# The first piece's block-diagonal copies, all on VectorE instead of shared with ScalarE

## The chip, the cores and the metric

The kernel runs on one core of a Trainium2 chip. Its metric is the device time of one launch, in microseconds (us). The engines of a core have their own instruction queues and work them off in order: PE (TensorE, matrix products; PEld is its weight load), DVE (VectorE), ACT (ScalarE), POOL (GpSimd) and SP, which here only issues DMA transfers. An instruction that needs another engine's result waits on a semaphore, and everything behind it in its own queue waits with it.

## The reference

A chunked scan (a state-space layer with decay) over 4 batches of 8 heads and 768 positions is followed by two feed-forward layers over 3072 tokens of width 256 with 2048 hidden features:

```python
for c in range(nc):                       # chunks of 32 positions
    L = np.exp(cum[:, :, :, None] - cum[:, :, None, :]) * causal
    M = np.einsum('bhin,bhjn->bhij', Cc, Bc) * L
    y_intra = np.einsum('bhij,bhjd->bhid', M, xc)
    y_inter = np.einsum('bhin,bhnd->bhid', Cc, state) * np.exp(cum)[..., None]
    y[:, :, sl] = y_intra + y_inter
    state = decay_full * state + np.sum(Bx, axis=2)
...
h = x @ w_in;   x = np.maximum(0.01 * h, h) @ w_out       # first layer
h = np.maximum(x @ w2_in, 0.0);   return h * h @ w2_out   # second layer
```

## The kernel before

**The scan.** The 3072 tokens are taken as 12 pieces of 256 positions (`scan_piece`, p from 0 to 11). A piece holds 8 heads as 2 groups of 4; the 4 heads lie on the four 32-partition quadrants of the 128 partitions. So that one matrix product serves four heads, operands are laid out block-diagonally: the nested function `diag` (L314 to L320) copies each quadrant of a source into its own column block of a 128 x 128 matrix, 16 such matrices side by side. There are four such arrays per piece: `kbd` from `kmx` (keys), `xbh` and `xbl` from `xh` and `xl` (the high and low halves of x), `sbd` from the transposed states. For pieces 1 to 11 the four copies of an array are DMAs. For piece 0 they are instructions: quadrants 0 and 1 on VectorE, 2 and 3 on ScalarE.

The chain of a piece: scales (squares on ACT at L235, a small product on PE at L290, some tiny DVE instructions from L298), decays by scans on DVE (L189, L195), `kbd` and `xbh`, products S on PE (L348, L349), the mask on DVE (L358), `mkh` on ACT (L360) and `mkl` on DVE (L365), products Y on PE (L373 to L375), states (ACT L377, DVE scan L213, ACT L382, DVE L384 and transpose L386), `sbd`, products L393 and L394, and the piece's result as a high half `yh` (ACT L397) and a low half `yl` (DVE L398).

**The layers.** The tokens go through both layers in 8 blocks, four of one piece and four of two. Each block has 16 hidden tiles of 128 features, taken two at a time in a small block. `hmm` (L417) makes `hp` on PE from `yl`, `yh` and the weights; `act` makes `gh` and `t` on ACT (L435, L436) and `gl` on DVE (L441); `omm` (L445) adds up the outputs `o`. Piece 0's `yl` releases block 0's first `hp`, and piece 1's `yl` block 1's first `hp`.

**The weights** arrive as 64-bit words and are split into two parts while the first pieces run. Of every chunk `wst` (512 KB, 32 chunks; 8 of them are w1i) ACT runs L130 and L133, DVE L141 and L142, ACT L153 (the high part, as `wh1i`) and DVE L154 (the low part, as `wl1i`).

**What sets the order.** The program is written as one sequence: the first piece's scan, eight rounds of weight splitting, then blocks with scan steps in between (`step_to`). From it the language's scheduler settles at build time which instruction stands where on each engine. Where an instruction is put on another engine, instructions far from it can change places too.

Of the kernel before, what the change touches and what calls it, by code (L numbers as in the profile page):

```python
# [45 lines left out]
def ssd_moe_kernel(ctx: ExitStack, tc: tile.TileContext, in1, in2, w1i, w1o, w2i, w2o, out):  # L46
# [6 lines left out]
    nc = tc.nc  # L53
# [254 lines left out]
    def scan_piece(p, tiles, get_y):  # L308
# [5 lines left out]
        def diag(dst, src):  # L314
            for h in range(4):
                d, v = dst[quad[h], :, h, :], src[quad[h]]
                if p > 0:
                    nc.sync.dma_start(d, v)  # L318
                else:
                    (nc.vector.tensor_copy if h < 2 else nc.scalar.copy)(d, v)  # L320

        him = sp.tile([P, U, T], F16, tag="f0", name="him")
        ch = sp.tile([P, U, T], F16, tag="f2", name="ch")
# [6 lines left out]
        cl = sp.tile([P, U, T], F16, tag="f3", name="cl")  # L330
        nc.vector.scalar_tensor_tensor(kmx, bt_t, sb, him, ALU.mult, ALU.subtract)
        diag(kbd, kmx)
        xh = sp.tile([P, U, D], F16, tag="xh", name="xh")
        nc.scalar.activation(xh, x_t, AF.Copy, scale=sx)
# [5 lines left out]
        xl = sp.tile([P, U, D], F16, tag="xl", name="xl")  # L340
        nc.vector.scalar_tensor_tensor(xl, x_t, sx, xh, ALU.mult, ALU.subtract)
        diag(xbh, xh)
        yield
        mkh = sp.tile([P, U, T + N], F16, tag="mkh", name="mkh")
        mkl = sp.tile([P, U, T + N], F16, tag="mkl", name="mkl")
        S = pz.tile([P, U, T], F32, tag="S", name="S")
        for u in range(U):
# [6 lines left out]
            mk[:, :, T:], b_t, sb, lt[:, :, T - 1 : T].to_broadcast([P, U, N]), ALU.mult, ALU.mult  # L354
        )
        diag(xbl, xl)
        yield
        nc.vector.scalar_tensor_tensor(mk[:, :, :T], S, kk, lt, ALU.mult, ALU.mult)  # L358
# [261 lines left out]
```

## Time and profile before

| | |
|---|---|
| Runs | 635.60, 636.33, 636.08 us; median 636.08 us |
| Profiled execution | 637.78 us, of which the span of the profile is 636.1 us |
| PE busy | 586.2 us, 92% of the span |
| PEld busy | 516.9 us, 81% |
| DVE busy | 402.6 us, 63%, 687 instructions |
| ACT busy | 372.9 us, 59%, 678 instructions |
| POOL busy | 5.2 us, 1% |

Shares over the whole span hide the stages. The page's row of 40 slices shows DVE and ACT at 9 tenths or more in the first slices, where PE is at 0 to 9, and PE at 9 in nearly all slices after the first third, where DVE and ACT are at 3 to 6. The chain of waits on the page gives PE 76%, ACT 9%, DVE 6% and DMA 6% of the span.

### The profile page before, as it was taken

How to read it: one execution, taken by the hardware profiler on the slowest of the kernel's cores; microseconds unless marked ns; L12 is line 12 of the kernel's file. 1: busy time of each engine (PE TensorE's matmuls, PEld its weight loads, DVE VectorE, ACT ScalarE, POOL GpSimd, SP SyncE). 2: the span in 40 equal slices, each digit the busy share in tenths (PEclk: the TensorE clock that was granted, in tenths of full speed). 3: DMA queues.
4: the chain of work that ended last, by engine and by line, in shares of the span. 5: the costliest groups of instructions: out<-in, count | busy, mean ns of one | idle time of the engine just before them, and what ended most of it. 6: DMA issues, size and time to landing. Idle time of an engine off the chain costs nothing.

```text
span 636.1 us, 11298 instructions
## 1 busy us (share of the span) xinstructions
PE 586.2 (92%) x4434; PEld 516.9 (81%) x4434; DVE 402.6 (63%) x687; ACT 372.9 (59%) x678; POOL 5.2 (1%) x14
## 2 busy tenths in 40 slices
PE   0297698999989999999999999999999999999997
PEld 0287698989989888899988888888888888888885
DVE  6999999995558664576564576564565322555553
ACT  6999998876555545545545555455544433544442
POOL 3000000000000000000000000000000000000000
PEclk9999898999989999999999999999999999999999
DMA  7886565555351412202212212212000000000000
GB/s 272 275 291 195 139 205 98 174 124 127 105 94 40 74 51 26 50 35 42 51 51 26 49 36 25 51 67 26 9 1 9 34 1 1 0 2 0 34 1 33
DMA packets 111396, 46.47 MB, mean 73 GB/s; under 512 B 94320, under 2 KB 101104, under 8 KB 111344
## 3 DMA queue, kind: packets, MB, share of 16 engines
q1 hardware_dynamic: 111344, 45.76, 27.8%
q8 instruction: 35, 0.57, 0.4%
q14 instruction: 17, 0.14, 0.1%
HBM read 36.83 MB, written 3.15 MB: 63 GB/s over the span
## 4 chain that ended last, share of the span: by engine, by line
PE 76%; ACT 9%; DVE 6%; DMA 6%; issue 2%; SPq 1%; DVEq 0%; ACTq 0%
PE o L453 12%; PE hp L425 12%; PE hp L427 12%; PE hp L426 12%; PE o L458 12%; PE o L454 12%; DMA all<-in 2%; DMA in<-in 2%; ACT wst L130 1%; ACT wst L133 1%; ACT sq L235 1%; SPq L318 1%; ACT t L436 1%; ACT gh L435 1%; DVE e L195 1%
## 5 line engine op out<-in xcount | busy, mean ns | idle before, releaser
L441 DVE TENSOR_TENSOR gl<-t,gh 128x512 fp32r<-128x512 f32 x192 | 132.3, 689 | 139.5 <-ACT t L436 85.9
L435 ACT ACTIVATE gh<-hp 128x512 fp32r<-128x512 f32 x96 | 57.2, 596 | 84.1 <-PE o L454 75.6
L425 PE MATMUL hp<-yl,wh1i 128*128 128x256 f32 (+1 forms) x256 | 89.5, 350 | 10.8 <-DVE yl L398 4.6
L440 ACT CAST gh<-t 128x512 fp32r<-128x512 f32 x96 | 59.5, 620 | 66.3 <-DVE t L439 56.2
L439 DVE TENSOR_TENSOR t<-t 128x512 f32<-128x512 f32 x96 | 66.2, 689 | 43.4 <-ACT t L438 43.1
L438 ACT ACTIVATE t<-hp 128x512 f32<-128x512 f32 x96 | 57.4, 598 | 56.7 <-PE hp L427 54.5
L453 PE MATMUL o<-gh,wl1o 128*128 128x256 f32 (+1 forms) x256 | 84.9, 347 | 4.5 <-DVE wl1o L154 3.6
L426 PE MATMUL hp<-yh,wh1i 128*128 128x256 f32 (+1 forms) x256 | 88.6, 346 | 0.0
L427 PE MATMUL hp<-yh,wl1i 128*128 128x256 f32 (+1 forms) x256 | 88.4, 345 | 0.0
L426 PE MATMUL hp<-yh,wh2i 128*128 128x256 f32 (+1 forms) x256 | 86.0, 336 | 0.0
L425 PE MATMUL hp<-yl,wh2i 128*128 128x256 f32 (+1 forms) x256 | 86.0, 336 | 0.0
L427 PE MATMUL hp<-yh,wl2i 128*128 128x256 f32 (+1 forms) x256 | 86.0, 336 | 0.0
L453 PE MATMUL o<-gh,w2o 128*128 128x256 f32 (+1 forms) x256 | 83.6, 343 | 1.6 <-DVE yl L467 1.5
L454 PE MATMUL o<-gh,wh1o 128*128 128x256 f32 (+1 forms) x256 | 83.0, 340 | 0.0
L454 PE MATMUL o<-gh,w2o 128*128 128x256 f32 (+1 forms) x256 | 81.9, 336 | 0.0
L425 PEld LDWEIGHTS hp<-yl,wh1i 128*128 128x128 f32 x256 | 51.3, 200 | 16.7 <-DVE ss L256 3.8
L458 PE MATMUL o<-gl,wh1o 128*128 128x256 f32 (+1 forms) x256 | 60.5, 339 | 0.0
L458 PE MATMUL o<-gl,w2o 128*128 128x256 f32 (+1 forms) x256 | 60.3, 336 | 0.0
L453 PEld LDWEIGHTS o<-gh,wl1o 128*128 128x128 f32 x256 | 48.9, 191 | 10.6 <-DVE wl1o L154 4.7
L436 ACT ACTIVATE t<-hp 128x512 f32<-128x512 f32 x96 | 57.1, 594 | 0.0
L426 PEld LDWEIGHTS hp<-yh,wh1i 128*128 128x128 f32 x256 | 51.3, 200 | 5.1 <-issue 0.3
L427 PEld LDWEIGHTS hp<-yh,wl1i 128*128 128x128 f32 x256 | 51.0, 199 | 5.1
(123 smaller groups left out, 984.8 us busy)
## 6 DMA issues: line engine op xcount, KB each, us to landing
in<-in SPq DMA_DIRECT2D x12, 640.0 KB, 4.6
in<-in SPq DMA_DIRECT2D x12, 512.0 KB, 3.4
all<-in SPq DMA_DIRECT2D x15, 384.0 KB, 3.7
wst<-w1i SPq DMA_DIRECT2D x8, 512.0 KB, 7.9
wst<-w1o SPq DMA_DIRECT2D x8, 512.0 KB, 5.8
wst<-w2o SPq DMA_DIRECT2D x8, 512.0 KB, 5.1
wst<-w2i SPq DMA_DIRECT2D x8, 512.0 KB, 4.7
out_t<-ob SPq DMA_DIRECT2D x8, 256.0 KB, 2.2
```

Of the source, the lines that this page charges most:

```text
L425: nc.tensor.matmul(hp, wh, self.xl[:, :, k], start=(k == 0), stop=False)
L426: nc.tensor.matmul(hp, wh, self.xh[:, :, k], start=False, stop=False)
L427: nc.tensor.matmul(hp, wl, self.xh[:, :, k], start=False, stop=(k == KI - 1))
L435: nc.scalar.activation(gh, hp, AF.Lrelu)
L436: nc.scalar.activation(t, hp, AF.Lrelu)
L438: nc.scalar.activation(t, hp, AF.Relu)
L439: nc.vector.tensor_tensor(t, t, t, ALU.mult)
L440: nc.scalar.copy(gh, t)
L441: nc.vector.tensor_tensor(gl, t, gh.bitcast(F32), ALU.subtract)
L453: nc.tensor.matmul(self.o[d], wl, gh, start=(m == 0), stop=False)
L454: nc.tensor.matmul(self.o[d], wh, gh, start=False, stop=False)
L458: nc.tensor.matmul(self.o[d], wh, gl, start=False, stop=(m == KO - 1))
```

## The change

```diff
@@ -317,7 +317,7 @@
                 if p > 0:
                     nc.sync.dma_start(d, v)
                 else:
-                    (nc.vector.tensor_copy if h < 2 else nc.scalar.copy)(d, v)
+                    nc.vector.tensor_copy(d, v)
```

`diag` is called four times for piece 0, so eight copies of 32 x 512 values (16 bits each) leave ScalarE and eight are added on VectorE. Pieces 1 to 11 use the same DMAs as before. The built order changes on PE, DVE, ACT and SP, not on POOL. Three places of it follow.

On DVE, from the decay scan of piece 0 (L189) to the mask of piece 0 (L358). `lt` is the scan's result, `kmx`, `xh` and `xl` the sources, `in` the input tile in which the mask is made. Before:

```order
L189 SCALAR_TENSOR_TENSOR lt<-in_117,delta 128x512
L320 COPY xbl<-xl 32x16x32
L353 SCALAR_TENSOR_TENSOR in_117<-in_116,sc,lt 128x16x16
L320 COPY xbl<-xl 32x16x32
L368 SCALAR_TENSOR_TENSOR ql<-e_179,sc,qh 128x512
L358 SCALAR_TENSOR_TENSOR in_117<-S,kk,lt 128x16x32
```

Now, in the same stretch:

```order
L189 SCALAR_TENSOR_TENSOR lt<-in_117,delta 128x512
L320 COPY kbd<-kmx 32x16x32 x2
L320 COPY xbh<-xh 32x16x32 x2
L353 SCALAR_TENSOR_TENSOR in_117<-in_116,sc,lt 128x16x16
L320 COPY xbl<-xl 32x16x32 x4
L358 SCALAR_TENSOR_TENSOR in_117<-S,kk,lt 128x16x32
```

Six copies more stand between the scan and the mask, and `ql` (L368) went behind the mask. The other two of the eight stand at `sbd`, where four copies follow each other in place of two. Ahead of piece 0's `yl` (L398) stand four L142 where six stood.

On ACT, from the first `gh` of block 0 on: `hp_421` and `hp_501` are the first and the second product of the block, `wst_355` and `wst_363` the last two of the eight chunks of w1i, `wst_395` a later chunk. Before:

```order
L435 ACTIVATE gh_435<-hp_421 128x512
L153 ACTIVATE wh1i_110<-wst_355 128x2x256
L153 ACTIVATE wh1i_110<-wst_363 128x2x256
L436 ACTIVATE t_434<-hp_421 128x512
L235 ACTIVATE sq_441,mx_440<-in1_290 128x256
L130 ACTIVATE wst_395<-wst_395 128x512
```

Now:

```order
L435 ACTIVATE gh_435<-hp_421 128x512
L436 ACTIVATE t_434<-hp_421 128x512
L435 ACTIVATE gh_515<-hp_501 128x512
L130 ACTIVATE wst_395<-wst_395 128x512
L153 ACTIVATE wh1i_110<-wst_355 128x2x256
L153 ACTIVATE wh1i_110<-wst_363 128x2x256
```

The two L153 moved from behind the first `gh` to behind the second one. On DVE the instructions that take their results (L154 of the same two chunks) are preceded, after piece 0's `yl`, by L142 twice, L141 twice, L154 twice, L142 twice and L141 once. The squares of piece 1 (L235), which stood behind the first `t`, went ahead, into the scan of piece 0.

On DVE, around piece 1's `yl`. The names with 738, 739 and 1038 belong to piece 2; `ss`, `iss`, `kk`, `fac` and `rr` are its scales. The difference of the two orders:

```order
 L189 SCALAR_TENSOR_TENSOR lt<-in_739,delta 128x512
-L398 SCALAR_TENSOR_TENSOR yl<-Y,fac,yh 128x512
 L256 TENSOR_SCALAR ss<-er 128x1
 L257 TENSOR_SCALAR iss<-er 128x1
-L331 SCALAR_TENSOR_TENSOR kmx<-in_739,sc,him 128x512
+L195 SCALAR_TENSOR_TENSOR e_1038<-in_739,d1e 128x512
+L398 SCALAR_TENSOR_TENSOR yl<-Y,fac,yh 128x512
 L259 TENSOR_TENSOR kk<-ss,u__925 128x1
 L261 TENSOR_TENSOR fac<-iss,isc 128x1
 L265 TENSOR_TENSOR rr<-ss,iss 128x1
-L195 SCALAR_TENSOR_TENSOR e_1038<-in_739,d1e 128x512
+L331 SCALAR_TENSOR_TENSOR kmx<-in_739,sc,him 128x512
```

Piece 1's `yl` went behind two tiny instructions and one scan (L195) of piece 2. Apart from these three and the copies, the same work stands ahead of it in both orders: among it 18 L141, 18 L142, 17 L154 and 8 `gl`.

On PE both orders put block 0's 96 `hp` and 96 `o` matmuls, and the products of pieces 0 and 1, ahead of block 1's first `hp`. On SP one of the last two w1i loads went from ahead of piece 1's second input load (L177) to behind it, and one `xbh` copy of piece 1 ahead of its `kbd` copies.

## Rows read from the trace of the kernel before

**Rows 1.** Busy time by stage: stretch, its length, PE, PEld, DVE, ACT, POOL, PEclk, DMA.
```profile
12.00:73.00 61.00, 36.11 (x420) 33.36 (x420) 59.95 (x125) 60.87 (x118) 0.00 (x0) 1.00 0.75 237
...
80.00:120.00 40.00, 37.48 (x407) 36.78 (x406) 38.07 (x70) 35.28 (x66) 0.00 (x0) 0.96 0.63 170
120.00:210.00 90.00, 83.57 (x911) 82.53 (x911) 64.84 (x112) 57.59 (x110) 0.00 (x0) 0.98 0.41 97
210.00:632.00 422.00, 421.91 (x2664) 357.24 (x2660) 225.72 (x347) 206.29 (x362) 0.00 (x0) 1.00 0.14 28
```

**Rows 2.** The chain of waits up to 80 us: start, time, what.
```profile
9.43 0.72 ACT ch L325
...
72.77 0.64 DVE yl L398
...
73.48 0.37 PE hp L425
```

**Rows 3.** Timeline of PE, block 0's and block 1's first hp: start, time, instruction, idle.
```profile
31.65 0.58 PE L425 MATMUL hp<-yl,wh1i 128*128 128x256 f32 x1 [2.45 <-DVE yl L398]
...
73.46 0.39 PE L425 MATMUL hp<-yl,wh1i 128*128 128x256 f32 x1 [3.68 <-DVE ss L256]
```

**Rows 4.** Instructions of line 320: duration ns min/median/max, first and last start.
```profile
L320 ACT COPY xbl<-xl x2: 610/612/613, 13.2 to 14.9; 32x512 f16<-32x512 f16 x2
L320 DVE COPY kbd<-kmx x2: 283/283/283, 13.3 to 13.6; 32x512 f16<-32x512 f16 x2
```

**Rows 5.** Timeline of DVE, 13 to 75 us.
```profile
13.34 0.58 DVE L320 COPY kbd<-kmx 32x512 f16<-32x512 f16 x2
...
16.26 0.75 DVE L368 SCALAR_TENSOR_TENSOR ql<-e,sc,qh 128x512 f16<-128x512 f32 x1 [0.21 <-ACT qh L366]
...
23.05 0.76 DVE L213 TENSOR_TENSOR_SCAN stt<-dec,d1s 128x288 f32<-128x288 f32 x1 [0.25 <-ACT d1s L377]
...
30.85 0.74 DVE L398 SCALAR_TENSOR_TENSOR yl<-Y,fac,yh 128x512 fp32r<-128x512 f32 x1
...
36.12 1.29 DVE L154 TENSOR_TENSOR wl1i<-wst,wh1i 128x512 fp32r<-128x512 f32 x2 [0.17 <-ACT wh1i L153]
...
72.68 0.72 DVE L398 SCALAR_TENSOR_TENSOR yl<-Y,fac,yh 128x512 fp32r<-128x512 f32 x1
...
73.39 0.14 DVE L257 TENSOR_SCALAR iss<-er 128x1 int32<-128x1 int32 x1
...
74.31 1.22 DVE L195 TENSOR_TENSOR_SCAN e<-in,d1e 128x512 f32<-128x512 f32 x1
```

**Rows 6.** Timeline of ACT around the first gh of block 0.
```profile
34.94 0.58 ACT L435 ACTIVATE gh<-hp 128x512 fp32r<-128x512 f32 x1
35.41 1.25 ACT L153 ACTIVATE wh1i<-wst 128x512 fp32r<-128x512 f32 x2
```

**Rows 7.** Timeline of PE: one hp matmul of block 0, two pairs of block 1.
```profile
32.25 0.41 PE L427 MATMUL hp<-yh,wl1i 128*128 128x256 f32 x1
...
73.80 0.28 PE L427 MATMUL hp<-yh,wl1i 128*128 128x256 f32 x1
73.92 0.28 PE L425 MATMUL hp<-yl,wh1i 128*128 128x256 f32 x1
...
74.75 0.41 PE L427 MATMUL hp<-yh,wl1i 128*128 128x256 f32 x1
74.97 0.41 PE L425 MATMUL hp<-yl,wh1i 128*128 128x256 f32 x1
```

**Rows 8.** Busy time, as in Rows 1, right after block 1's first matmuls.
```profile
74.30:77.60 3.30, 3.30 (x18) 3.30 (x17) 3.24 (x8) 2.69 (x6) 0.00 (x0) 0.50 0.74 148
```

**Rows 9.** Timeline of SP: piece 1's second input load.
```profile
20.38 0.33 SPq L177 DMA_DIRECT2D in<-in  x1
```

**Rows 10.** Timeline of PE: the longest waits after 80 us.
```profile
104.89 0.51 PE L425 MATMUL hp<-yl,wh1i 128*128 128x256 f32 x1 [2.16 <-DVE yl L398]
...
179.75 0.18 PE L393 MATMUL Y<-qh,sbd 128*128 128x32 f16 x1 [2.93 <-DMA sbd<-t]
```

## The prediction

> **What bounds the kernel now.** I first read busy time by stage [rows 1]. From 210 us on PE is busy 421.91 of 422.00 us, so every microsecond that block work starts late reaches the end, unless an idle stretch of PE before that takes it up. From 12 to 73 us it is otherwise: PE is busy 36.11 of 61.00 us, while DVE has 59.95 and ACT 60.87. Two engines are full at once there, and the question is which of them PE waits for.
>
> The chain of waits starts on ACT (9.43) and goes over to DVE shortly before block 1: piece 1's `yl` at 72.77, then `hp` at 73.48 [rows 2]. The timeline of PE shows the same [rows 3]: block 0's first `hp` starts at 31.65 after 2.45 us of idle that DVE's `yl` ends, block 1's at 73.46 after 3.68 us. The latter row names `ss`, a tiny instruction just behind `yl` on DVE. So DVE opens both gates, and the reader should note that each is the end of a full queue: whatever is added to DVE ahead of it comes out at PE.
>
> **The change part by part.**
>
> ACT loses eight copies of 0.61 us, 4.9 us in all; DVE gains eight of 0.283 us [rows 4]. Two on the same array take 0.58 us together on DVE, so they start 0.30 apart [rows 5]; I take 0.29 each, 2.3 us.
>
> How much of this fits into DVE's idle time? Between 12 and 73 us there are 1.05 us of it (61.00 less 59.95) [rows 1], and three waits for ACT make up 0.21 + 0.25 + 0.17 = 0.63 of that [rows 5]. ACT, relieved, would be earlier at all three. I credit 0.6, within 0 and 1.05.
>
> *First gate.* Ahead of piece 0's `yl` stand eight copies more and two L142 fewer. An instruction of the split takes 0.60 from start to start (two take 1.29, one about 0.69) [rows 5]. So `yl` moves by 2.3 less 1.2 less the first two waits, 0.46: +0.6 us, from 30.85 to about 31.5, and block 0 starts on PE at 31.65 + 0.6 = 32.3 [rows 3, 5]. What ACT saves does not bring this gate forward: `yl` stands behind DVE's own copies.
>
> *A wait that the new order adds.* ACT's L153 of the last two w1i chunks now stands behind the second `gh`, which needs 24 `hp` matmuls of block 0. How fast these run depends on the clock. In block 1 two neighbours start 0.12 us apart before 74.3, and one matmul is 0.28 us long; from 74.3 to 77.6, right after PE's idle 3.68 us, the granted clock is 0.50 (the 1.2 GHz level), they start 0.22 apart and one is 0.41 long [rows 3, 7, 8]. Early in block 0 one is 0.41 long too [rows 7], so I take 0.22 there, less a little for rounding: 0.215. Then the 24 end at 32.3 + 5.2 = 37.5. ACT needs 0.47 for `gh` (to the next start), 0.58 for L130, which has the size of L153, and 0.67 for the first L153 (two take 1.25) [rows 6], and is done at 39.2. DVE comes to the L154 that needs this after `yl` (0.7) and nine instructions of 0.60: 31.5 + 0.7 + 5.4 = 37.6. It waits 1.6 us. If the clock is up for the last matmuls it is a few tenths less; were all at 0.12, PE would be done at 35.2, ACT at 36.9, and there would be no wait. I take 1.4, with 0 and 1.6 as ends. Behind the waiting L154 stand all later splits, `gl` and the scan of piece 1, so it counts in full.
>
> *Second gate.* Apart from this, the work ahead of piece 1's `yl` on DVE is the same set, plus one scan L195 and two tiny instructions of piece 2. The scan takes 1.22 us by itself, a tiny one 0.14 [rows 5]; neighbours overlap a little, so together they hold the queue for about 1.2, with 1.5 (1.22 + 2 x 0.14) as the upper end and 0 as the lower, should `yl` wait for ACT's `yh` anyway.
>
> The sum at the second gate: 2.3 - 0.6 + 1.4 + 1.2 = **4.3 us**. Block 1's first `hp` goes from 73.46 to about 77.8. The same 192 matmuls of block 0 stand ahead of it, so PE has nothing to fill the longer gap with.
>
> *Does it wash out later?* PE idles 2.5 us from 80 to 120 (40.00 less 37.48) and 6.4 from 120 to 210 [rows 1]. The first large one, 2.16 us at 104.89, again ends with a DVE `yl`, and DVE is full there, with 38.07 of 40 [rows 1, 10]. The largest, 2.93 at 179.75, waits for the DMA of `sbd`, whose source comes from ACT and DVE instructions that stand in order among the `gh` and `gl` of running blocks; they move with the blocks. I let nothing be absorbed, and 6.4 + 2.5 bounds what could be.
>
> *DMA.* One of the last two w1i loads is now issued behind piece 1's second input load, at 20.38 before [rows 9], some us later than its place ahead of it. Its splits are the last of w1i, and ACT, with 4.9 us less to do, has room for it: 0, at most 1 us. The reordered `xbh` DMA of piece 1 stands well before the product that reads it: 0.
>
> The profiled execution has 637.78 us with a span of 636.1; with 4.3 more it would be 642.1. It stands 1.7 above the median of the runs, so I put the 4.3 on the median: 636.08 + 4.3 = **640.4 us**.
>
> *The Trainium skill on this.* Perfetto Trace Analysis, Optimizing Scalar/DVE Operations, says that a DVE with a fast mode does an operation faster than Scalar, but that with DVE saturated it may pay to hand work to Scalar. The first half agrees with 0.283 against 0.61 us [rows 4]; the second half speaks against this change, and 59.95 of 61.00 us on DVE [rows 1] is such a state. By the price of a copy alone one would forecast a gain, by the state of the queue a loss; I follow the queue.
>
> **The rivals.**
>
> *ACT is the bound, and the kernel gets faster.* ACT is fuller than DVE by 0.9 us from 12 to 73 [rows 1], and the chain runs on it early [rows 2]. If DVE's copies found room and ACT set the pace, the second gate would come forward by up to 4.9 - 2.3 = 2.6 us: 633.5. It decides from the point where DVE has more than 2.3 us of idle, and it has 1.05. Perfetto Trace Analysis, Identifying the Most-Contended Engine, would pick ACT by occupancy and have it relieved first; no row here shows PE released by ACT at either gate. Chance 0.06.
>
> *Only the copies count.* The wait behind the second `gh` does not come (PE at 0.12) and the L195 is hidden because `yl` waits for ACT anyway: 2.3 - 0.6 = 1.7, 637.8. For it: both are consequences of the order, worked out from starts that can slip. Chance 0.17.
>
> *Later gaps take it up.* If the gaps after 120 us end at times set by scans and DMAs that don't move, up to 6.4 us vanish: 636.1, no change. Against it is the in-order queue. Chance 0.09.
>
> *A further slow stretch of PE.* At 0.50 of the clock, 3.3 us cost 3.3 x (1 - 0.12/0.22) = 1.5 us [rows 7, 8]. The gap ahead of block 1 grows from 3.7 to about 4.6 us, and the gaps within block 0 shift; one more such stretch gives 4.3 + 1.5: 641.9. Chance 0.18.
>
> **How the numbers follow.** The forecast itself, 4.3 with 639.2 to 641.5 around it, has 0.50. A difference under 0.2% (1.3 us) can't be told from none for this kernel. Faster: 0.06, the first rival. Same: 0.09, and the lower end of "only the copies", together 0.11. Slower: 0.83. For eight in ten the range leaves out the first and the third rival and reaches from the lower side of the second, 637.2, to a slow stretch more with the high ends, 642.8.
>
> **What would show it right or wrong.** ACT should have idle time between 12 and 40 us that it lacks now, and DVE none but one wait of 1 to 2 us at an L154 near 39 us, ended by ACT's L153. Block 0's first `hp` should start near 32.3 and block 1's near 77.8, after a gap of over 4 us ended by DVE. The last 420 us of PE should look unchanged. The prediction fails at its root if block 0 starts before 31.5, since DVE then was not what `yl` waited for; at the added wait if DVE shows no idle near 39; at the carrying over if block 1 starts over 4 us late and the end does not.

## The result, and the profile after

The changed kernel takes 642.19 us in the median (640.68 to 642.86, four runs) against 635.84 for the kernel before on the same chip (634.73 to 636.33): ratio 1.0099, interval 1.0076 to 1.0122, so 6.3 us slower (4.8 to 7.8). The forecast was 640.4 within 637.2 to 642.8: right in its sign and within its range, with 4.3 us where 6.3 were measured; 642.19 lies nearer to the rival with a further slow stretch of PE (641.9). The profiled execution has 642.86 us with a span of 641.1, 5.0 above that of before. Of 22 executions of the kernel before that were timed beside later runs, those with a mean granted clock of 0.996 or more took 633.3 to 634.2 us and those with 0.989 or less 637.6 to 639.1, so two single profiles can differ by microseconds for this alone.

Busy time by stage of the changed kernel; the columns are those of [rows 1].

```profile
12.00:73.00 61.00, 36.26 (x381) 33.34 (x382) 58.35 (x119) 55.73 (x107) 0.00 (x0) 0.95 0.72 223
80.00:120.00 40.00, 37.46 (x372) 36.82 (x372) 35.95 (x69) 30.17 (x56) 0.00 (x0) 0.91 0.61 155
120.00:210.00 90.00, 85.96 (x935) 85.08 (x932) 66.22 (x114) 60.26 (x115) 0.00 (x0) 0.98 0.42 107
210.00:632.00 422.00, 420.92 (x2691) 357.23 (x2691) 228.09 (x351) 208.27 (x366) 0.00 (x0) 1.00 0.14 28
```

ACT is busy 5.1 us less in the first stretch. DVE, which was to be fuller, is emptier (58.35 against 59.95), although it has eight copies more to do by its gate: it now waits. From 210 us on the work is the same; the 1.1 us that PE idles there is a wait for `sbd` that both kernels have (1.05 at 214.41, before 1.11 at 209.33).

The three gates of PE (timeline of PE: start, time, instruction, idle time before it and what ended it), and the longest wait later:

```profile
32.57 0.58 PE L425 MATMUL hp<-yl,wh1i 128*128 128x256 f32 x1 [2.09 <-DVE yl L398]
...
79.38 0.58 PE L425 MATMUL hp<-yl,wh1i 128*128 128x256 f32 x1 [4.29 <-DVE yl L398]
...
111.10 0.55 PE L425 MATMUL hp<-yl,wh1i 128*128 128x256 f32 x1 [2.35 <-DVE yl L398]
...
186.17 0.18 PE L393 MATMUL Y<-qh,sbd 128*128 128x32 f16 x1 [1.47 <-DMA sbd<-t]
```

Against [rows 3, 10] the first gate is 0.9 us late, the second 5.9, the third 6.2. So nearly all of the loss is there at 111 us. What follows in these two executions is the clock and one wait. The changed kernel has a stretch at half clock (0.50, the 1.2 GHz level) from 145.2 us on, where before has none, and piece 3's `yl` is 8.0 us late; at the wait for `sbd` the idle time shrinks from 2.93 to 1.47, which leaves 6.4; and behind that wait the kernel before has such a stretch, the changed one none, which leaves 5.1 from 212 us on. Before (first row) and changed kernel (second row):

```profile
180.00:183.40 3.40, 3.40 (x41) 3.40 (x38) 2.95 (x5) 1.79 (x4) 0.00 (x0) 0.50 0.40 43
145.20:148.60 3.40, 3.40 (x18) 3.40 (x17) 2.39 (x4) 0.62 (x1) 0.00 (x0) 0.50 0.66 142
```

The loss up to 111 us arises on DVE, whose timeline shows what follows (rows of its waits between the first two `yl`):

```profile
31.77 0.75 DVE L398 SCALAR_TENSOR_TENSOR yl<-Y,fac,yh 128x512 fp32r<-128x512 f32 x1
...
35.43 1.29 DVE L154 TENSOR_TENSOR wl1i<-wst,wh1i 128x512 fp32r<-128x512 f32 x2 [0.51 <-ACT wh1i L153]
...
39.40 1.29 DVE L154 TENSOR_TENSOR wl1i<-wst,wh1i 128x512 fp32r<-128x512 f32 x2 [0.87 <-ACT wh1i L153]
...
44.90 0.69 DVE L154 TENSOR_TENSOR wl1o<-wst,wh1o 128x512 fp32r<-128x512 f32 x1 [0.31 <-ACT wh1o L153]
...
77.47 1.21 DVE L195 TENSOR_TENSOR_SCAN e<-in,d1e 128x512 f32<-128x512 f32 x1
78.60 0.72 DVE L398 SCALAR_TENSOR_TENSOR yl<-Y,fac,yh 128x512 fp32r<-128x512 f32 x1
```

And ACT, ahead of the L153 that DVE waits for:

```profile
34.15 0.71 ACT L130 ACTIVATE wst<-wst 128x512 f32<-128x512 f32 x1 [1.63 <-DMA wst<-w1o]
...
37.40 0.61 ACT L435 ACTIVATE gh<-hp 128x512 fp32r<-128x512 f32 x1
38.13 0.68 ACT L130 ACTIVATE wst<-wst 128x512 f32<-128x512 f32 x1
38.71 1.23 ACT L153 ACTIVATE wh1i<-wst 128x512 fp32r<-128x512 f32 x2
```

A ledger of DVE up to the `yl` that opens a gate says how much is work and how much is waiting. For the kernel before (columns as in [rows 1]; the stretches end where the second and the third `yl` start):

```profile
12.00:72.68 60.68, 36.11 (x420) 33.36 (x420) 59.63 (x124) 60.55 (x117) 0.00 (x0) 1.00 0.75 237
12.00:104.00 92.00, 65.02 (x728) 61.58 (x728) 89.63 (x184) 89.38 (x171) 0.00 (x0) 0.98 0.71 213
```

and for the changed kernel:

```profile
12.00:78.60 66.60, 38.35 (x420) 35.27 (x420) 63.62 (x135) 61.19 (x117) 0.00 (x0) 0.94 0.70 218
12.00:110.21 98.21, 67.53 (x728) 63.83 (x728) 92.52 (x193) 86.78 (x165) 0.00 (x0) 0.93 0.68 200
```

To the second `yl`: 5.92 us more, of which 3.99 are work (63.62 less 59.63) and 1.93 waiting (2.98 less 1.05). To the third: 6.21 more, 2.89 work and 3.32 waiting (5.69 less 2.37). So between the two gates 1.1 us of extra work goes out of the balance again, and waiting comes in its place.

### The profile page after: what moved, and what is told of

The parts are those of the page before. It is cut to its first block, busy times and chain, and to the rows that moved or that the text cites. A ratio compares the mean times of both kernels' runs of the same rounds, so it can differ in the third digit from the quotient of the medians.

```text
span 641.1 us, 11293 instructions
## 1 busy us (share of the span) xinstructions
PE 588.9 (92%) x4434; PEld 519.3 (81%) x4434; DVE 404.4 (63%) x695; ACT 369.1 (58%) x670; POOL 5.2 (1%) x14
## 4 chain that ended last, share of the span: by engine, by line
PE 76%; DVE 10%; DMA 6%; ACT 5%; issue 2%; SPq 1%; DVEq 0%; ACTq 0%
PE o L453 12%; PE hp L425 12%; PE o L454 12%; PE o L458 12%; PE hp L426 12%; PE hp L427 12%; DMA wst<-w2o 2%; DMA wst<-w1o 2%; DMA in<-in 1%; DVE e L195 1%; DVE lt L189 1%; SPq L318 1%; DVE gl L441 1%; ACT sq L235 1%; ACT wst L130 1%
## 5 line engine op out<-in xcount | busy, mean ns | idle before, releaser
L435 ACT ACTIVATE gh<-hp 128x512 fp32r<-128x512 f32 x96 | 57.3, 597 | 85.7 <-PE o L454 75.6
L425 PE MATMUL hp<-yl,wh1i 128*128 128x256 f32 (+1 forms) x256 | 89.3, 349 | 13.4 <-DVE yl L398 8.7
L427 PE MATMUL hp<-yh,wl1i 128*128 128x256 f32 (+1 forms) x256 | 88.2, 345 | 0.0
L425 PE MATMUL hp<-yl,wh2i 128*128 128x256 f32 (+1 forms) x256 | 86.4, 338 | 0.0
L427 PE MATMUL hp<-yh,wl2i 128*128 128x256 f32 (+1 forms) x256 | 86.4, 338 | 0.0
L425 PEld LDWEIGHTS hp<-yl,wh1i 128*128 128x128 f32 x256 | 51.0, 199 | 19.5 <-DVE yl L398 6.6
L436 ACT ACTIVATE t<-hp 128x512 f32<-128x512 f32 x96 | 57.0, 594 | 0.0
L453 PEld LDWEIGHTS o<-gh,w2o 128*128 128x128 f32 x256 | 48.6, 190 | 8.0 <-DVE yl L467 2.3
L427 PEld LDWEIGHTS hp<-yh,wl1i 128*128 128x128 f32 x256 | 50.8, 199 | 5.1
```

The costliest lines, as they stand in the source:

```text
L425: nc.tensor.matmul(hp, wh, self.xl[:, :, k], start=(k == 0), stop=False)
L427: nc.tensor.matmul(hp, wl, self.xh[:, :, k], start=False, stop=(k == KI - 1))
L435: nc.scalar.activation(gh, hp, AF.Lrelu)
L436: nc.scalar.activation(t, hp, AF.Lrelu)
L453: nc.tensor.matmul(self.o[d], wl, gh, start=(m == 0), stop=False)
```

## The experiments

The theory was that DVE's queue sets the gates and each microsecond ahead of `yl` is carried to the end. The rivals were that ACT is the bound, that the gates do not carry, and that the order, which is laid out anew as soon as one instruction changes its engine, is the cost rather than the copies. Each kernel was timed in five rounds beside the kernel before, and the ratios are to that. In the first four the order is laid out anew. Lines that a run adds to the kernel shift the line numbers in its rows: `hp` is L425 in before and L427 or L474 in some runs. Pieces are counted from 0 here, as in the prediction; where piece 1 and 2 are meant, some expectations say first and second piece.

**Half of the copies left out.**

```diff
-                    (nc.vector.tensor_copy if h < 2 else nc.scalar.copy)(d, v)
+                    if h < 2:
+                        nc.vector.tensor_copy(d, v)
```

> The eight copies leave ScalarE and are made by nobody: quadrants 2 and 3 of the first piece's four block-diagonal arrays stay zero, so that part of the computation is left out. DVE makes its eight as before, and ACT is relieved of 4.9 us. In its built order the scan L195 of piece 2 again stands ahead of piece 1's yl, as in the changed kernel. Theory 'DVE's queue': the relief of ACT buys nothing beyond the 0.6 us that DVE waited for ACT, and L195 costs 1.2, so block 0 starts on PE near 31.0 and block 1 near 74.5, and the time is 636 to 637.5. Rival 'ACT is the bound': 4.9 us less on ACT brings both gates forward by 2.6 to 4.9, 631 to 633.5. Rival 'the new order alone costs the time': 640 or more, since the order moved as in the changed kernel.

Ratio 1.0006 (0.9987 to 1.0024). Taking 4.9 us of work from ACT, and giving it to nobody, gains nothing in the order that comes with it. PE's second and third gate:

```profile
75.47 0.58 PE L426 MATMUL hp<-yl,wh1i 128*128 128x256 f32 x1 [4.29 <-DVE yl L399]
...
106.88 0.36 PE L426 MATMUL hp<-yl,wh1i 128*128 128x256 f32 x1 [1.19 <-DVE yl L399]
```

Both come 2.0 us late, 1.0 more than expected for the second, and still the time is that of before: here, in an order that differs behind the gates too, their lateness is not carried. The Trainium skill, Perfetto Trace Analysis, Identifying the Most-Contended Engine, would relieve the engine with the highest occupancy first; that was ACT by 60.87 to 59.95 [rows 1], and in this run that gained nothing.

**VectorE's own copies made twice, ScalarE's kept.**

```diff
                     (nc.vector.tensor_copy if h < 2 else nc.scalar.copy)(d, v)
+                    if h < 2:
+                        nc.vector.tensor_copy(d, v)
```

> ACT makes its eight copies as before; DVE makes its own eight twice, so it has eight copies more and nothing is taken from ACT. The output is the same. In its built order L195 of piece 2 stays behind piece 1's yl. Theory 'DVE's queue': the eight copies alone move the gates by 2.3 us less up to 0.5 of idle, block 1 starts on PE near 75.5, and the time is 637.8 to 639. Rival 'ACT is the bound': DVE's copies fit beside ACT's work, 636 +- 1. Rival 'the loss needs the new order (L195, the wait behind gh)': under 637.4.

Ratio 0.9982 (0.9969 to 0.9996): not slower, against the theory. Its timeline of PE:

```profile
76.17 0.39 PE L427 MATMUL hp<-yl,wh1i 128*128 128x256 f32 x1 [3.62 <-DVE ss L256]
...
107.39 0.36 PE L427 MATMUL hp<-yl,wh1i 128*128 128x256 f32 x1 [1.42 <-DVE yl L400]
...
177.34 0.18 PE L395 MATMUL Y<-qh,sbd 128*128 128x32 f16 x1 [1.15 <-DMA sbd<-t]
```

The second gate is 2.7 us late and the third 2.5, as eight copies on DVE would have it; at the `sbd` wait the kernel is 2.4 us early (177.34 against 179.75 [rows 10]). The theory holds up to 107 us and the carrying over does not, in an order that was laid out anew beyond that point too.

**ScalarE's eight copies on GpSimd.**

```diff
-                    (nc.vector.tensor_copy if h < 2 else nc.scalar.copy)(d, v)
+                    (nc.vector if h < 2 else nc.gpsimd).tensor_copy(d, v)
```

> Quadrants 2 and 3 are copied by GpSimd, which is idle after 6 us, quadrants 0 and 1 by DVE as before; ACT is relieved of 4.9 us and nothing is left out. In its built order L195 stays behind piece 1's yl. A 32 x 512 cast on GpSimd takes 0.61 us at line 88 of the trace of before. Theory 'DVE's queue': DVE has what it had, so block 1 starts between 72.5 and 73.5 and the time is 635 to 636. Rival 'ACT is the bound': 631 to 633.5. Rival 'what ACT saves is spent waiting for weight loads that DVE has to free, and the order that comes with it costs time later': slower than before by 1 us or more with block 1 starting no later than 73.5.

Ratio 1.0104 (1.0080 to 1.0127), as slow as the changed kernel, though DVE has no copy more; the second gate is at 77.04, where 72.5 to 73.5 was expected. That speaks for the order, or for a price of GpSimd's copies; a later run parts the two.

**The changed kernel with piece 2's scan pinned behind piece 1's `yl`.**

```diff
-        nc.vector.tensor_tensor_scan(e1.rearrange(fl), az.rearrange(fl), d1e.rearrange(fl), 0.0, ALU.mult, ALU.add)
+        sc_ = nc.vector.tensor_tensor_scan(e1.rearrange(fl), az.rearrange(fl), d1e.rearrange(fl), 0.0, ALU.mult, ALU.add)
+        if p == 2:
+            tc.add_manual_dep(sc_.ins, last["yl"].ins.name, mybir.DependencyInfo(mybir.DependencyClass.NoSync, mybir.DependencyReason.DATA), reason="order")
```

(Shortened: `p` is also handed in, and `last["yl"]` is set where `yl` is made.)

> The changed kernel with one order pinned: the scan L195 of piece 2 is issued behind piece 1's yl, as in the kernel before; no wait is added. Theory 'DVE's queue': block 1 starts 1.2 us earlier than the 79.38 us of the changed kernel, near 78.2, and the time is 1.2 less, about 641. Rival 'the gate does not carry to the end': block 1 starts earlier and the time stays at 642. Rival 'the order is most of the loss': 638 or less.

Ratio 1.0059 (1.0038 to 1.0080), some 2.5 us under the changed kernel. The second gate is at 78.18, as expected. But the one edge lays out much else anew, so this does not price the scan.

The next eight hold every engine to a given order. A table names the instructions of VectorE, ScalarE, SyncE and TensorE up to the last place where the two kernels' orders differ, and each is tied behind the one ahead of it (order of issue alone, no wait is added; the cut is shortened):

```diff
+    traced = {i.name: i for i in nc.cur_bb.bb.instructions}
+    for text in FORCED.values():
...
+        for first, then in zip(names, names[1:]):
+            tc.add_manual_dep(traced[then], first, mybir.DependencyInfo(mybir.DependencyClass.NoSync, mybir.DependencyReason.DATA), reason="order")
```

**The copies alone: changed kernel, order of before.** FORCED is the order of before, and on VectorE (172 to 175 `kbd`, 184 to 187 `xbh`, 225 to 228 `xbl`, 299 to 302 `sbd`):

```diff
-184 157 159 171 185 172 173 168 225 224 226 ... 299 300
+184 157 159 171 185 186 187 172 173 174 175 168 225 224 226 227 228 ... 299 300 301 302
```

> The eight copies are VectorE's as in the changed kernel, but every engine is held to the order of the kernel before (each moved copy stands on VectorE right behind the copy of its own diag call that stood there already). Theory 'VectorE's queue' (8 copies at 0.29 us, less at most 0.6 us of idle time that they fill): the second block's first hp about 1.7 to 2.3 us later than 73.46, and the total 1.7 to 2.3 us above the kernel before, ratio 1.0027 to 1.0036. Rival 'the new order is the cost, the copies alone are absorbed': second block's first hp up to 2.3 us late, the total within 0.2% of before (ratio 0.998 to 1.002). Rival 'ScalarE was the bound': faster, ratio 0.996.

Ratio 1.0034 (1.0014 to 1.0053): 2.2 us. PE's gates and DVE's ledger:

```profile
33.83 0.58 PE L474 MATMUL hp<-yl,wh1i 128*128 128x256 f32 x1 [2.69 <-DVE yl L447]
...
75.65 0.58 PE L474 MATMUL hp<-yl,wh1i 128*128 128x256 f32 x1 [3.75 <-DVE ss L305]
```

```profile
12.00:74.87 62.87, 36.14 (x420) 33.76 (x420) 61.88 (x131) 56.84 (x109) 0.00 (x0) 0.99 0.72 227
12.00:106.93 94.93, 65.83 (x728) 62.77 (x728) 91.82 (x192) 85.73 (x163) 0.00 (x0) 0.96 0.68 205
```

Both gates are 2.2 us late. DVE's work up to the second is 2.25 more (61.88 less 59.63), its waiting the same (0.99 against 1.05), although ACT has 3.7 us less to do by then (56.84 against 60.55). That is the price of the copies at the gates, and the times, which are 2.2 us apart as well (0.9 to 3.4), say that it is carried. The two traces don't show this last step: in this execution the `sbd` wait ends 1.0 us late, and the spans are equal to 0.2 us, since the trace of before has the longer wait there (2.93, here 1.17) and the half clock behind it.

**The order alone: kernel before, order of the changed one.** The diff is that of ScalarE's row in FORCED against the changed kernel's order (names as above; 340 to 346: L130, L133; 295: L382; 365: L153). ScalarE's copies stand behind the same ScalarE instruction as in before; the two of `sbd`, whose source comes later in this order, behind the L153 that follows the cast L382.

```diff
-162 340 345 346
+162 186 187 227 174 175 228 340 345 346
...
-295 365 446
+295 365 301 302 446
```

> ScalarE makes its eight copies as in the kernel before, but every engine is held to the order of the changed kernel. Theory 'VectorE's queue': the loss of 6.3 us less the copies' 2.3, so 3.5 to 4 us above before (ratio 1.0055 to 1.0065), or more, where ScalarE's copies of 0.6 us each (4.9 us in all) now stand in an order that was laid out without them. Rival 'the new order is the cost': at least the whole loss, 6.3 us or more (ratio 1.0095 or more). Rival 'the copies on VectorE are the cost': within 0.2% of before.

Ratio 1.0150 (1.0122 to 1.0177): 9.5 us. DVE's waits ahead of its first `yl`, and the ledger to the third:

```profile
17.87 0.75 DVE L415 SCALAR_TENSOR_TENSOR ql<-e,sc,qh 128x512 f16<-128x512 f32 x1 [0.94 <-ACT qh L413]
...
21.86 0.96 DVE L412 TENSOR_TENSOR mkl<-in,mkh 128x768 f16<-128x768 f32 x1 [2.64 <-ACT mkh L407]
...
34.40 0.69 DVE L201 TENSOR_TENSOR wl1i<-wst,wh1i 128x512 fp32r<-128x512 f32 x1 [1.90 <-ACT wh1i L200]
```

```profile
12.00:112.80 100.80, 65.95 (x728) 62.19 (x728) 90.34 (x185) 91.03 (x173) 0.00 (x0) 0.97 0.66 195
```

The four timings side by side, in us against before:

| | ScalarE makes half | VectorE makes all |
|---|---|---|
| order of before | 0 | +2.2 |
| order of the changed kernel | +9.5 | +6.3 |

In the new order handing the copies over is worth 3.2 us, since that order was laid out for an ACT without copies: with them, the three waits above add 5.5 us ahead of the first `yl` alone. How much they add depends on where in the order the copies are put, and one place was tried. In the old order the relief of ACT is worth nothing and the copies cost their 2.2. The change brings the copies and the order: 2.2 and, taken after them, 4.1 (by the intervals of the two ratios some 2 to 6). Taken first, the order alone is 9.5, so the two prices are not a plain sum. At the third `yl` the ledgers of the changed kernel and of the one with the copies alone differ by 3.3 us, 0.7 of work and 2.6 of waiting (5.69 against 3.11).

**GpSimd's copies in the order of before.** The kernel of the run with GpSimd, with FORCED as the order of before.

```diff
-                    (nc.vector.tensor_copy if h < 2 else nc.scalar.copy)(d, v)
+                    (nc.vector if h < 2 else nc.gpsimd).tensor_copy(d, v)
```

> ScalarE's eight copies are made by GpSimd, and every engine is held to the order of the kernel before. In the earlier run with GpSimd (order laid out anew, ratio 1.0104) VectorE's copies beside GpSimd's took 0.60 to 0.69 us in place of 0.28, and the L189 scan 1.56 in place of 1.22. If that is its price, the first block's first hp comes 2 to 3 us late and the total is 2 to 3 us above before (ratio 1.003 to 1.005), with the other 4 us of that run being the order. Rival 'ScalarE's relief pays for it': within 0.2% of before or faster. Rival 'the order did not matter': 1.0104 again.

Ratio 1.0048 (1.0027 to 1.0069), 3 us, against 1.0104 with the order laid out anew: there, too, the order costs some 3.6 us. Most of the 3 us arise on DVE, whose second `yl` starts at 74.98, 2.3 us late. Its timeline:

```profile
13.10 0.28 DVE L368 COPY xbh<-xh 32x512 f16<-32x512 f16 x1
13.39 1.27 DVE L368 COPY kbd<-kmx 32x512 f16<-32x512 f16 x2
14.70 1.56 DVE L237 TENSOR_TENSOR_SCAN lt<-in,delta 128x512 f32<-128x512 f32 x1
16.18 0.63 DVE L368 COPY xbl<-xl 32x512 f16<-32x512 f16 x1
```

GpSimd's copies run from 13.21 to 18.35, those of `sbd` from 28.61 on. Before they start, one of DVE's takes 0.28; beside them 0.63, and two 1.27 in place of 0.58 [rows 5].

**One place of the order turned back: the split ahead of the second `gh`.** In the changed kernel's order, on ScalarE (397, 405: L153; 437, 517: L435; 438: L436):

```diff
-437 438 517 497 397 405 498
+437 397 405 438 517 497 498
```

> The changed kernel in its own order, with one thing turned back: ScalarE's L153 of the last two w1i chunks stands ahead of its second gh (L435) again, as in the kernel before. If the wait near 39 us is worth what was predicted, the second block's first hp comes 1.4 us sooner than 79.38 and the total is 1.4 us under the changed kernel (ratio to before 1.0099 - 0.0022 = 1.0077). Rival 'VectorE waits at L154 there, but catches the wait up or has it from the late weight loads instead': under 0.4 us, ratio to before 1.009 to 1.0105.

Ratio 1.0115 (1.0089 to 1.0141): no gain. The second gate of PE stays where it was in the changed kernel (79.38). On DVE the wait at 39.40 is gone, and DVE waits elsewhere:

```profile
79.28 0.39 PE L473 MATMUL hp<-yl,wh1i 128*128 128x256 f32 x1 [4.32 <-DVE yl L446]
```

```profile
42.23 0.69 DVE L202 TENSOR_TENSOR wl1o<-wst,wh1o 128x512 fp32r<-128x512 f32 x1 [0.74 <-ACT wh1o L201]
43.83 0.69 DVE L202 TENSOR_TENSOR wl1o<-wst,wh1o 128x512 fp32r<-128x512 f32 x1 [0.32 <-ACT wh1o L201]
...
56.58 0.75 DVE L406 SCALAR_TENSOR_TENSOR in<-S,kk,lt 128x512 f32<-128x512 f32 x1 [1.15 <-PE S L397]
```

**Another: piece 2's scan behind piece 1's `yl`.** On VectorE (933, 934: L256, L257; 1039: L195; 862: `yl`):

```diff
-990 933 934 1039 862 936
+990 862 933 934 1039 936
```

> The changed kernel in its own order, with one thing turned back: the second piece's L195 and the two small L256 and L257 stand behind the first piece's yl (L398) on VectorE again. If their placing is worth what was predicted, the second block's first hp comes 1.2 us sooner (78.2) and the total is 1.2 us under the changed kernel (ratio to before 1.008). Rival 'it also moves the half-clock stretch': up to 2.5 us under it (ratio 1.006), as the version with a re-laid order did. Rival 'later gaps take it up': no difference from the changed kernel (1.0099).

Ratio 1.0100 (1.0068 to 1.0132), no difference that could be told. PE's second and third gate:

```profile
76.87 0.39 PE L473 MATMUL hp<-yl,wh1i 128*128 128x256 f32 x1 [3.50 <-DVE ss L304]
...
109.48 0.36 PE L473 MATMUL hp<-yl,wh1i 128*128 128x256 f32 x1 [2.35 <-DVE yl L446]
```

The second gate comes 2.5 us sooner: up to `yl` DVE has 1.6 us less of work (62.00 for 63.62) and 0.9 less of waiting (2.10 for 2.98). At the third gate 1.6 are left. The interval reaches 2 us either way, so these 1.6 may or may not be in the time. A wait that came in between stands on ACT, just ahead of piece 2's cast `mkh`, for which DVE then waits 1.21 us:

```profile
82.00 0.84 ACT L283 ACTIVATE sq<-all 128x768 bf16<-128x768 f32 x1 [0.26 <-DMA all<-in]
...
87.36 0.84 ACT L283 ACTIVATE sq<-all 128x768 bf16<-128x768 f32 x1 [1.40 <-DMA all<-in]
```

The loads of `all` share one buffer: the next is issued when the squares have read the last (here at 82.97) and is there 4.4 us later.

**A third: weight loads ahead on SyncE.** (364: last w1i load, 293: L177, 372 to 420: w1o, 911: L276, 1861 and 1870: w2o)

```diff
-356 293 364 372 911 380 388 1861 396 1870 404 412 420
+356 364 372 293 380 388 396 404 412 420 911 1861 1870
```

> The changed kernel in its own order, with SyncE's queue alone laid out so that weight loads stand ahead of what is not needed soon: the last w1i load and the first w1o load ahead of L177, the load of all (L276) and the two early w2o loads behind the w1o loads. Theory 'ScalarE's 2.2 us of waiting for w1o loads in the changed kernel (1.6 at 34.15, 0.6 at 42.04) is what idles VectorE at L154': those waits go, VectorE's idle time between the first two yl falls from 2.6 to about 0.7 us, the second block's first hp comes 1.9 us sooner than 79.38 and the total 1.9 us under the changed kernel (ratio to before about 1.007). Rival 'the loads are late because their buffers come free late (VectorE's L154 of the chunk before), not because of what stands ahead of them': no change, ratio 1.0099, hp at 79 to 79.5.

Ratio 1.0089 (1.0066 to 1.0112), which the intervals don't tell from the changed kernel's 1.0099; the second gate comes 0.5 us sooner, at 78.88, where 77.5 was expected. ACT's waits for weight loads fall from 2.2 us to 0.3, and DVE's two waits of 0.51 and 0.87 become one of 1.90, since ACT's second `gh` still waits for PE until 37.98:

```profile
39.72 1.29 DVE L202 TENSOR_TENSOR wl1i<-wst,wh1i 128x512 fp32r<-128x512 f32 x2 [1.90 <-ACT wh1i L201]
```

**All three turned back.** The three edits above in one kernel:

```diff
-437 438 517 497 397 405 498
+437 397 405 438 517 497 498
-990 933 934 1039 862 936
+990 862 933 934 1039 936
-356 293 364 372 911 380 388 1861 396 1870 404 412 420
+356 364 372 293 380 388 396 404 412 420 911 1861 1870
```

> The changed kernel in its own order with three things turned back together: loads (as in the run on SyncE's queue), the split of the last two w1i chunks (L153) ahead of the second gh, and the second piece's L195, L256 and L257 behind the first piece's yl. Theory 'these hold the cost of the new order': of the 5.9 us at the second block's first hp 1.9 (idle time) and 1.3 (L195 and two small ones) go, so 76.2, and the total is 2.5 to 3 us above before (ratio 1.004 to 1.0047), as with the old order and the copies alone (1.0034). Rival 'the order costs through something else': ratio 1.007 or more, hp at 77.5 or later.

Ratio 1.0108 (1.0087 to 1.0129): nothing gained, the rival's side. PE's gates, and DVE and ACT between them:

```profile
76.90 0.47 PE L473 MATMUL hp<-yl,wh1i 128*128 128x256 f32 x1 [3.44 <-DVE ss L304]
...
111.10 0.47 PE L473 MATMUL hp<-yl,wh1i 128*128 128x256 f32 x1 [2.34 <-DVE yl L446]
```

```profile
89.67 0.96 DVE L413 TENSOR_TENSOR mkl<-in,mkh 128x768 f16<-128x768 f32 x1 [1.80 <-ACT mkh L408]
```

```profile
87.98 0.84 ACT L283 ACTIVATE sq<-all 128x768 bf16<-128x768 f32 x1 [2.00 <-DMA all<-in]
```

The second gate is 2.5 us sooner, the third at the same time as in the changed kernel, 111.10. The chain through the loads of `all` is the same as with the scan alone turned back, with 5.0 us from the issue (82.98) to the squares and 1.80 of waiting on DVE behind `mkh`. It is about half of DVE's 3.7 us of waiting between the two `yl`; the rest is for PE and ACT.

**The gate opened sooner in the kernel before.** Order of before, with piece 1's `yh` (861) and `yl` (862) moved ahead on ScalarE and VectorE (944, 1001: L325, L334; 986 to 988, 928, 1004, 932, 990: L185 to L187, L251, L336, L255, L189):

```diff
-944 1001 861
+861 944 1001
-986 987 928 988 1004 932 990 862
+862 986 987 928 988 1004 932 990
```

> The kernel before in its own order (ScalarE still makes its eight copies), with one thing moved: the first piece's yh (L397) ahead of the second piece's ch and xh on ScalarE, and its yl (L398) ahead of the second piece's L185 to L189, L251, L336 and L255 on VectorE. If whatever delays or hastens the second block's first hp is carried to the end, as the prediction has it: yl starts at about 70.8 in place of 72.68, hp at 71.6 in place of 73.46, and the total is 1.9 us under before (ratio 0.997). Rival 'the third gap (102.73 to 104.89) gives it back, since the second piece's scan now runs 0.7 us later': ratio 0.999 to 1.002. Rival 'the gap ends sooner, so a stretch at half clock goes too': 3 us or more under before (ratio 0.995).

Ratio 0.9993 (0.9973 to 1.0013).

```profile
71.59 0.39 PE L473 MATMUL hp<-yl,wh1i 128*128 128x256 f32 x1 [1.77 <-DVE yl L446]
...
104.32 0.35 PE L473 MATMUL hp<-yl,wh1i 128*128 128x256 f32 x1 [2.13 <-DVE yl L446]
```

The second gate comes at 71.59, 1.9 us sooner as expected; at the third 0.6 are left, and in the time nothing that can be told. DVE's work up to the second `yl` is 57.36 us in place of 59.63, and up to the third 89.35 in place of 89.63: what stands behind one gate is due before the next.

## Why the prediction was right, and where its sizes were off

*DVE opens the gates.* Right. All three gates between 31 and 111 us end with DVE's `yl` (or the tiny instruction right behind it), and in the order of before the gates move by DVE's own work (2.2 for 2.25 us), whatever ACT is relieved of.

*Eight copies, 2.3 us.* Right: 0.284 us each in the changed kernel, 2.25 us of work and 2.2 us of time when they alone are moved. The credit of 0.6 for DVE's idle time was not borne out there. Two of the three waits for ACT in [rows 5], 0.21 and 0.17, go in that run, the third stays and small new ones come, and the sum of the waiting does not move (1.05 to 0.99).

*First gate at 32.3.* It came at 32.57; 0.24 of the 0.46 us of waiting that were credited there went (0.62 to 0.38).

*The added wait, 1.4 us.* It was there, where it was put: the second `gh` runs at 37.40 (forecast 37.5), ACT's L153 ends at about 39.3 (forecast 39.2), DVE waits 0.87 at 39.40. It came there 0.51 late by a wait at 35.43 that was not forecast, so the two make 1.38 together; without the first, as with the loads ahead, it waits 1.90 in one place. But the cause that was named does not carry the price. With the L153 back in its old place the second gate stays (79.28), since DVE's waiting turns up at other instructions: ACT and DVE hand work to and fro, and what one is behind shows at whichever hand-over comes next.

*L195 ahead of `yl`, 1.2 us.* About right at the second gate (with it and the two tiny ones turned back, 1.6 us of work go), and wrong as a term of the sum to the end. It is work moved, not added, and at the third `yl` it is done in either order: the surplus of work falls from 3.99 to 2.89 us. Turned back, it brings the second gate forward by 2.5 us, and the third, with the wait behind the loads of `all` in between, by 1.6 in one run and by nothing in the other. "I let nothing be absorbed" failed here, 30 us on, for which the prediction had only the full DVE as evidence. In the changed kernel this hardly shows in the total, because 1.4 us of new waiting stand between the two gates (2.71 against 1.32). That the two cancel is luck.

*DMA, 0.* ACT waited 2.2 us for w1o loads, more than the bound of 1. Taking these waits away moved the second gate by 0.5 us, the third by 0.9 and the time by 0.1%, less than can be told: no run speaks against a price of 0 to 1, but the mechanism was not seen.

*No absorption after 80 us.* The `sbd` wait took up 1.5 us (2.93 to 1.47) in the profiled execution, of the 7.9 (6.4 and 1.5) that PE was late by then. "Later gaps take it up" was partly right there, and more so in two runs with an order of their own: with half of the copies left out and with VectorE's copies made twice the second and third gate are 2.0 to 2.7 us late and the time is not longer. Where the order behind the gates is that of before or that of the changed kernel, a late second and third gate goes with a longer time. Why the other two lose it again was not tried.

*A further stretch at half clock.* In the changed kernel there are two around the second gate (its stretches as in [rows 8]), where there was one of 3.4 us:

```profile
66.70:73.40 6.70, 5.63 (x25) 5.21 (x26) 6.70 (x15) 6.70 (x16) 0.00 (x0) 0.50 0.66 162
76.90:83.70 6.80, 4.32 (x20) 4.32 (x21) 5.53 (x14) 5.24 (x11) 0.00 (x0) 0.50 0.52 91
```

The first is over before DVE opens the gate, so nothing of it shows there; of the second, 4.3 us lie behind the gate at 79.38, 1.0 more than in [rows 8], or 0.5 us by the rate of the prediction. Later each execution has one stretch behind the third gate, and one more that stands at 145 us in the changed kernel and at 180 in before. The granted clock differs between executions of one kernel (0.985 to 0.997 for before), so how much of the 6.3 us such stretches are is not shown.

So the sum was 4.3 with copies 1.7 (2.3 less 0.6), and 2.6 for the order; measured are 6.3 with 2.2 and 4.1. The mis-sized term is the order's, and neither of its two parts carries it: turned back together with the loads they left the time at 1.0108. Up to the third `yl` 3.3 of the 4.1 us are seen, 0.7 us of work and 2.6 of waiting on DVE, spread over waits of 0.2 to 1.3 us for ACT and PE. Which positions of the new order bring these about is open: three candidates turned back, singly and together, did not remove them. The three chunks whose first split (L130, L133) the new order puts ahead of piece 1's `yh` on ACT, and the chain through the loads of `all`, were not tried by themselves.

None of the versions is a gain worth having. The kernel with VectorE's copies made twice is 0.2% under before (0.9982), and as those copies only add work, the gain can only be its order's; no run holds that order with the copies taken out.

## What to carry to other kernels

Where a scheduler lays out the queues, moving eight small instructions to another engine is two changes: the instructions and a new order. Hold the old order fixed in one run and the new order in another, and the two come apart; here the copies cost what their durations say, and the order on top of them about twice as much. On a full in-order queue count what is added and what is waited for up to each gate in turn; what merely changes sides of one gate is due at the next, and a gate that opens sooner need not bring the next one forward: here 1.9 us became 0.6, and 2.5 became 1.6 and 0. One profile of each kernel is not enough to follow such a loss to the end, as stretches at half clock fall differently from execution to execution.

## What the runs showed of the hardware that had not been expected

GpSimd's copies slow VectorE's down. A 32x512 copy on VectorE takes 0.28 us, and 0.59 to 0.69 beside GpSimd's; the L189 scan takes 1.56 us in place of 1.22. Work handed from ScalarE to GpSimd so cost VectorE 2.7 us up to the second gate (62.32 us of work against 59.63), more than making the eight copies itself (2.25):

```profile
12.00:74.98 62.98, 35.49 (x420) 32.82 (x420) 62.32 (x126) 56.70 (x109) 6.45 (x8) 1.00 0.72 227
```

The Trainium skill, Perfetto Trace Analysis, Optimizing Scalar/DVE Operations, says that GpSimd and VectorE share a read port into SBUF and that handing work between those two may not help; these rows agree in that VectorE's copies take twice their time beside GpSimd's; that the port is the reason they do not show.
